# A linear-attention and MLP kernel on one core: exponentials and logarithms by halves of the heads, and another order of the whole program

## The chip, the core and the metric

The kernel runs on one core of one Trainium2 chip. The core has a matrix engine (PE, whose weight loads the profile lists apart as PEld), a vector engine (DVE), an activation engine (ACT), a general engine (POOL) and a sequencer that issues transfers (SP). They run side by side and wait for each other through semaphores. The metric is the time of one execution on the device in microseconds (us), as the median of several runs.

## The reference

Two stages follow each other. The first is a gated linear attention over 4 batches, 8 heads, 768 steps and 48 channels a head; the second is an MLP with SiLU over the 3072 tokens that the first gives, with 384 columns and 2048 hidden units.

```python
f = 1.0 / (1.0 + np.exp(-f_logit))
for t in range(S):
    state = f[:, :, t, :, None] * state + np.einsum('bhd,bhe->bhde', k[:, :, t], v[:, :, t])
    y[:, :, t] = np.einsum('bhd,bhde->bhe', q[:, :, t], state)
# y as x: (tokens, H*D)
h = x @ w_in
g = h * (1.0 / (1.0 + np.exp(-h)))
return g @ w_out
```

## The kernel before

**Tiling.** The 768 steps are cut into 6 chunks of 128, so that there are 24 units (a chunk of a batch, all 8 heads), and two units make a pair. Pairs 0 to 2 are "blocks": their two units are two neighbouring chunks of one batch, and their f, k and q are loaded with two neighbouring steps in one row of 96 numbers. Pairs from 3 on are two batches of the same chunk, loaded in rows of 48.

**A unit's work.** The logits are loaded (`f`), put through exp (`E`) and ln (`L`), so that `lf` holds log(1+exp(-logit)). A matmul with a triangle of ones sums them along the steps (`csh` for a block, `cs` for a unit). From the sums ACT makes `ia` and `a` (exponentials of both signs) and `al` (the decay over the whole chunk). Products with them give scaled keys and queries (`ki`, `qg`), in `qk`. These are turned: in the early units on PE (`tq`, with copies `qc`, `kc` or `qkc`), later by a transposing DMA (`qkD`). `sc2` makes the scores of a pair, `at` masks them on DVE, `vb` casts the values, and `y` is the output: masked scores times values plus queries times the state of the chunk before. `d`, `sd` and `su` carry the state on (for blocks `dT` and `kn` turn the keys back first). `yc` copies y out, `yT` and `xc` (or the transposing DMA `yD`) turn it for the MLP.

**The MLP.** For the first units (`mi1`, `si1`) a matmul group makes 4 tiles of 128 hidden units for one unit, later (`mi`, `si`) 2 tiles for a pair; SiLU runs on ACT. `mo` is a quarter of the second matmul, `oc` copies the output and `so` stores it; the last pair is done by halves of the columns (`moh`, `och`, `soh`). The weights come in pieces: `wi_0` and `wi_1` are 256 columns of w_in each (384 KB), `wi_2` to `wi_4` 512 columns (768 KB), `wo_0` to `wo_3` a quarter of w_out each (768 KB). Every piece is cast to bf16 by three casts (`wic`, `woc`), two for the small ones. `mi1_u_0` needs `wi_0` and `wi_1`, `mi1_u_1` needs `wi_2`, `mi1_u_2` and `mi1_u_3` need `wi_3` and `wi_4`.

**Order.** Nothing is scheduled at build time. A table `PLAN` of some 890 words says, for all engines together, in what order the instructions are issued; a word is the task with its numbers, the engine, and the buffers that it takes (`mi1_0_1/PE/6`: first matmul of unit 0, hidden tiles 4 to 7, on PE, into bank 6 of the eight PSUM banks). Each engine works through its own words in that order and stands still at a word whose inputs or buffers aren't free. `idle_...` words are matmuls of zeros that only keep PE running before there is work. ACT loads another table of functions wherever the plan goes from exponentials to SiLU or back, which it does 17 times in both versions. Line 257 issues f, k, q and v on SP, line 295 w_in and line 299 w_out; line 264 is `E`, lines 266 and 268 `L`; lines 335 to 339 `csh`; line 313 `mi1`, line 323 `mi`, line 351 `mo`, line 357 `moh`; line 280 the scores; line 407 `qkD`, line 442 `yD`; lines 235, 237 and 239 are copies and casts on ACT, DVE and POOL, line 242 the products.

Of the kernel before, what the change touches and what calls it, by code (L numbers as in the profile page):

```python
# [36 lines left out]
kn_0/ACT/0 d_0/PE/2 wi_1/SP/0 wi_0/SP/1 at_0_1/DVE/0 at_0_0/DVE sd_0/DVE/0 at_1_0/DVE/1 su_0/POOL/0 idle_4_2_256/PE/1 y_0/PE/3 tq_3/PE/1,5
idle_5_2_256/PE/2 tq_2/PE/2,0 wo_0/SP/1 a_4/ACT/1 ia_5/ACT/1 al_4/ACT/2 kc_3/ACT/1 at_1_1/DVE qc_3/DVE vb_1/ACT/1 a_5/ACT/2 yc_0/ACT/0 ia_4/ACT/2
kc_2/DVE qc_2/DVE y_1/PE/7 dT_2/PE/5 yT_0/PE/1 sc2_1/PE/6,0,3,2 wo_1/SP/2 wic_2_2/POOL wic_2_0/POOL yc_1/DVE/1 wic_2_1/ACT vb_2/ACT/2 xc_0/DVE/0
at_2_0/DVE/2 at_2_1/DVE dT_1/PE/4 yT_1/PE/7 dT_3/PE/1 mi1_0_1/PE/6 wi_4/SP/3 y_2/PE/0 xc_1/ACT wic_1_0/ACT wic_0_0/ACT kn_1/DVE/1 kn_2/DVE/0  # L40
yc_2/DVE/2 at_3_0/DVE/3 wic_1_1/POOL wic_0_1/POOL mi1_1_1/PE/7 d_2/PE/4 yT_2/PE/5 mi1_0_0/PE/0 mi1_1_0/PE/3 wi_3/SP/4 si1_0_1/ACT/0 si1_1_0/ACT
si1_0_0/ACT sd_2/DVE/1 xc_2/DVE/1 woc_0_2/DVE woc_0_1/DVE woc_0_0/DVE v_3/SP woc_1_2/DVE mi1_2_1/PE/4 mi1_2_0/PE/5 mo_1_0/PE/6 mo_0_0/PE/3 d_1/PE/0
si1_2_1/ACT/1 si1_2_0/ACT kn_3/ACT/0 woc_1_0/POOL si1_1_1/ACT wic_4_0/POOL wic_4_1/POOL wic_4_2/ACT at_3_1/DVE woc_1_1/DVE su_2/DVE/0 wic_3_1/DVE
sd_1/DVE/0 wic_3_2/POOL mo_2_0/PE/4 q_4_5/SP/2 k_4_5/SP/2 mo_1_1/PE mo_0_1/PE mo_2_1/PE mi1_0_3/PE/5 mi1_2_3/PE/1 mi1_1_3/PE/2 wo_2/SP/0 wic_3_0/ACT
vb_3/POOL/3 mi1_1_2/PE/7 y_3/PE/0 si1_0_3/ACT si1_2_3/ACT si1_1_2/ACT yc_3/DVE/0 qg_4/POOL/4 wo_3/SP/1 mi1_2_2/PE/5 d_3/PE/1 ki_4/POOL sd_3/DVE/1
yT_3/PE/7 mi1_0_2/PE/0 si1_2_2/ACT si1_0_2/ACT xc_3/DVE tq_4/PE/5,1 mi1_3_3/PE/7 mi1_3_2/PE/0 kc_4/ACT/2 si1_1_3/ACT qc_4/DVE si1_3_3/ACT si1_3_2/ACT
qg_5/DVE/0 ki_5/POOL tq_5/PE/5,1 mi1_3_0/PE/2 mi1_3_1/PE/7 f_6/SP/3 v_4/SP/2 f_8_9/SP/0 v_5/SP f_7/SP qc_5/ACT si1_3_0/ACT si1_3_1/ACT woc_2_2/POOL
woc_2_0/DVE woc_2_1/DVE kc_5/DVE mo_2_2/PE sc2_2/PE/0,5,2,1 dT_4/PE/7 mo_0_2/PE at_5_1/DVE/0 su_3/DVE/0 su_1/DVE/0 kn_4/DVE/1 at_5_0/DVE at_4_0/DVE/1
# [482 lines left out]
```

## Time and profile before

| what | before |
|---|---|
| median of 3 runs | 177.57 us (177.55 to 178.02) |
| the profiled execution's own time | 177.89 us |
| its span in the trace | 176.1 us |
| PE busy | 169.5 us, 96% of the span |
| ACT busy | 133.3 us, 76% |
| DVE busy | 97.7 us, 55% |
| POOL busy | 59.1 us, 34% |
| table loads on ACT | 17 of 1.28 us |
| moved by DMA | 35.17 MB, of 115541 packets |

The span lies inside the profiled execution: 1.8 us of its time are around it. Busy time counts instructions that were under way, so that a PE that is busy 96% need not run at its peak; where PE waits is read from the starts of its instructions, and what ended a wait from the profile's releasers.

### The profile page before, as it was taken

How to read it: one execution, taken by the hardware profiler on the slowest of the kernel's cores; microseconds unless marked ns; L12 is line 12 of the kernel's file. 1: busy time of each engine (PE TensorE's matmuls, PEld its weight loads, DVE VectorE, ACT ScalarE, POOL GpSimd, SP SyncE). 2: the span in 40 equal slices, each digit the busy share in tenths (PEclk: the TensorE clock that was granted, in tenths of full speed). 3: DMA queues.
4: the chain of work that ended last, by engine and by line, in shares of the span. 5: the costliest groups of instructions: out<-in, count | busy, mean ns of one | idle time of the engine just before them, and what ended most of it. 6: DMA issues, size and time to landing. Idle time of an engine off the chain costs nothing.

```text
span 176.1 us, 4798 instructions
## 1 busy us (share of the span) xinstructions
PE 169.5 (96%) x1952; PEld 133.6 (76%) x1952; DVE 97.7 (55%) x201; ACT 133.3 (76%) x249; POOL 59.1 (34%) x91
## 2 busy tenths in 40 slices
...
DMA  5999998998999999999899994999675975950222
GB/s 147 325 286 259 397 387 220 397 207 169 217 199 241 182 238 221 159 233 232 152 197 165 251 227 89 273 176 210 137 153 99 206 162 138 217 147 0 92 90 89
DMA packets 115541, 35.17 MB, mean 200 GB/s; under 512 B 110752, under 2 KB 113056, under 8 KB 115520
## 3 DMA queue, kind: packets, MB, share of 16 engines
...
## 4 chain that ended last, share of the span: by engine, by line
PE 73%; SPq 8%; DMA 8%; DVE 5%; issue 2%; POOL 2%; ACT 0%; POOLq 0%; DVEq 0%
PE ps L351 27%; PE ps L323 22%; PE ps L313 8%; SPq L257 6%; DMA wh<-in_moe_w_in_dram 5%; PE ps L280 3%; PE ps L357 3%; DMA qkT<-qk 3%; PE ps L426 2%; SPq L442 2%; DVE st L242 2%; PE ps L422 2%; PE ps L372 1%; DVE at L416 1%; PE ps L448 1%
## 5 line engine op out<-in xcount | busy, mean ns | idle before, releaser
L351 PE MATMUL ps<-w_out,hT 128*128 128x384 bf16 x352 | 66.4, 326 | 0.0
L323 PE MATMUL ps<-xT,w_in 128*128 128x256 bf16 x432 | 52.4, 273 | 0.0
L323 PEld LDWEIGHTS <-w_in 128*128 128x128 bf16 x432 | 45.3, 110 | 3.9 <-DMA xT<-yb 0.3
L320 ACT ACTIVATE hT<-ps 128x512 bf16<-128x512 f32 x72 | 39.0, 603 | 10.3 <-PE ps L323 9.6
L351 PEld LDWEIGHTS <-hT 128*128 128x128 bf16 x352 | 31.7, 97 | 16.6 <-ACT hT L310 0.3
L416 DVE TENSOR_TENSOR at<-ps,triu 128x512 bf16<-128x512 f32 x36 | 22.5, 683 | 19.8 <-PE ps L280 18.8
L242 POOL TENSOR_TENSOR qk<-q,av 128x384 bf16<-128x384 f32 x15 | 15.4, 1033 | 42.2 <-DMA q<-in_q_dram 25.0
L499 ACT ACT_TABLE_LOAD x17 | 21.8, 1283 | 0.3
L313 PE MATMUL ps<-xT,w_in 128*128 128x128 bf16 x288 | 17.9, 219 | 0.9 <-POOL w_in L239 0.6
L313 PEld LDWEIGHTS <-w_in 128*128 128x128 bf16 x288 | 16.6, 110 | 1.3 <-POOL w_in L239 0.8
L242 POOL TENSOR_TENSOR qk<-k,ia 128x384 bf16<-128x384 f32 x12 | 12.7, 1066 | 13.4 <-DMA k<-in_k_dram 8.7
L381 ACT ACTIVATE av<-ps 128x384 f32<-128x384 f32 x24 | 11.9, 504 | 3.5 <-PE ps L376 1.8
L237 DVE CAST yb<-ps 128x384 bf16<-128x384 f32 x16 | 8.8, 555 | 10.2 <-PE ps L426 9.0
L264 ACT ACTIVATE f<-f 128x768 f32<-128x768 f32 (+1 forms) x13 | 10.3, 796 | 5.4 <-DMA f<-in_f_logit_dram 5.3
L310 ACT ACTIVATE hT<-ps 128x512 bf16<-128x512 f32 x24 | 13.2, 607 | 1.6 <-PE ps L313 1.5
L453 DVE TENSOR_TENSOR sd<-ps,st 128x384 f32<-128x384 f32 x16 | 8.8, 553 | 9.5 <-ACT hT L320 4.7
L369 POOL DMA_DIRECT2D out_dram<-ob x14 | 8.0, 573 | 17.9 <-DVE ob L237 14.3
L242 POOL TENSOR_TENSOR st<-sd,al 48x192 bf16<-48x192 f32 x18 | 9.8, 543 | 8.7 <-PE ps L422 5.1
L379 ACT ACTIVATE ia<-ps 128x384 f32<-128x384 f32 x24 | 11.8, 505 | 0.0
L237 DVE COPY ob<-ps 128x384 f32<-128x384 f32 x14 | 7.7, 553 | 7.4 <-PE ps L351 3.6
L239 POOL CAST vb<-v 128x384 bf16<-128x384 f32 x11 | 5.6, 507 | 14.6 <-DMA v<-in_v_dram 13.2
L242 DVE TENSOR_TENSOR qk<-k,ia 128x384 bf16<-128x384 f32 x12 | 7.1, 605 | 5.1 <-ACT ia L379 4.2
...
## 6 DMA issues: line engine op xcount, KB each, us to landing
...
```

What stands on the lines that cost most here:

```text
L237: nc.vector.tensor_copy(o, i)
L242: (nc.vector if eng == "DVE" else nc.gpsimd).tensor_mul(*a)
L257: nc.sync.dma_start(out=dst, in_=src)
L310: return nc.scalar.activation(at("hT", u // 2)[:, 4 * m:4 * m + 4, i * C:(i + 1) * C], h, AF.Silu)
L313: nc.tensor.matmul(h[:, n, :], w_in_tile(4 * m + n, kk), at("xT", u // 2)[:, kk, i * C:(i + 1) * C], start=(kk == 0), stop=(kk == KT - 1))
L320: return nc.scalar.activation(at("hT", P)[:, 2 * j:2 * j + 2, :], h, AF.Silu)
L323: nc.tensor.matmul(h[:, i, :], w_in_tile(2 * j + i, kk), at("xT", P)[:, kk, :], start=(kk == 0), stop=(kk == KT - 1))
L351: nc.tensor.matmul(o, at("hT", P)[:, n, i * C:(i + 1) * C], w_out_sb[n // 4][:, n % 4, :], start=(n == 0), stop=(n == NT - 1))
L379: nc.scalar.activation(at("ia", u).rearrange("p h d -> p (h d)"), at("cs", u)[:, 0:HD], AF.Exp)
L381: nc.scalar.activation(at("av", u).rearrange("p h d -> p (h d)"), at("cs", u)[:, 0:HD], AF.Exp, scale=-1.0)
L416: nc.vector.tensor_mul(at("at", u)[:, r], at(f"s{r}", u).rearrange("p (n c) -> p n c", c=C), (triup if two else triu)[:, None, :].to_broad ...
L499: nc.scalar.preload_act_table_set(turn[n])
```

## The change

Three things change in the code. First, the constant `HALF = 3` (the first three pairs are blocks) becomes a set `BLOCKS = {0, 1, 2}` with the same meaning. Second, two new kinds of task, `Eh` and `Lh`, do the exp and the ln of a block for four of the eight heads at a time; all three blocks use them, where one instruction did all heads before. Third, the plan is another one from its first word to its last. Code for transfers of half a block, for weights cast by a DMA of POOL and for the scores of a single unit (`sc`) comes in as well, but no word of the new plan uses it: each block of f is still one transfer. The buffers (`SLOTS`) are the same. The new plan has 10 `E` and 10 `L` of the old form and 6 `Eh` and 6 `Lh`.

```diff
-HALF = 3
+BLOCKS = {0, 1, 2}
...
-f_0_1/SP/0 f_2_3/SP/1 k_0_1/SP/0 q_0_1/SP/0 E_0_1/ACT L_0_1/ACT/0 E_2_3/ACT idle_0_11_512/PE/0 csh_0/PE/0,1 f_4_5/SP/2 q_2_3/SP/1 v_0/SP/0 k_2_3/SP/1
...
+wi_1/SP/1 dT_0/PE/5 kn_0/DVE/0 al_2/ACT/1 dT_2/PE/7 at_0_1/DVE vb_2/ACT/2 d_0/PE/1 Eh_4_1/ACT sd_0/DVE/0 idle_5_2_256/PE/2 y_0/PE/2 qc_3/ACT
...
-        "L": lambda: [(("lf", P), "lf")],
+        "L": lambda: [(("lf", P), "lf")], "Lh": lambda: [(("lf", P), "lf")],
...
-        if u // 2 < HALF and n == 2:
-            dst = at(x, u // 2).rearrange("p a h d -> p (a h d)").rearrange("p (h w) -> p h w", h=H)
-            src = SRC[x][b, :, c * C:(c + 2) * C, :].rearrange("h (p s) d -> p h (s d)", s=2)
+        if u // 2 in BLOCKS and n >= 2:
+            hs = slice(0, H) if n == 2 else slice(4 * us[2], 4 * us[2] + 4)
+            dst = at(x, u // 2).rearrange("p a h d -> p (a h d)").rearrange("p (h w) -> p h w", h=H)[:, hs]
+            src = SRC[x][b, hs, c * C:(c + 2) * C, :].rearrange("h (p s) d -> p h (s d)", s=2)
...
+    def half_logs(kind, u, hf):
+        P, hs = u // 2, slice(4 * hf, 4 * hf + 4)
+        if kind == "Eh":
+            e = at("f", P).rearrange("p a h d -> p (a h d)").rearrange("p (h w) -> p h w", h=H)[:, hs]
+            nc.scalar.activation(e, e, AF.Exp, scale=-1.0)
+        else:
+            nc.scalar.activation(at("lf", P)[:, :, hs, 0:D], pairs("f", P)[:, :, hs], AF.Ln, bias=1.0)
...
+        if kind in ("Eh", "Lh"):
+            return half_logs(kind, *a)
```

**SP, the opening.** The names are buffers: `f0` to `f2`, `k0`, `q0` and so on hold the blocks, `v0` and `v1` single units of v, `wh` the small pieces of w_in, `ws` the large ones. Before, the transfers start so:

```order
L257 DMA f0_69<-in_f_logit_dram 128x8x96
L257 DMA f1_70<-in_f_logit_dram 128x8x96
L257 DMA k0_73<-in_k_dram 128x8x96
L257 DMA q0_77<-in_q_dram 128x8x96
L257 DMA f2_71<-in_f_logit_dram 128x8x96
L257 DMA q1_78<-in_q_dram 128x8x96
L257 DMA v0_81<-in_v_dram 128x8x48
L257 DMA k1_74<-in_k_dram 128x8x96
L257 DMA v1_82<-in_v_dram 128x8x48
L257 DMA v0_81<-in_v_dram 128x8x48
L295 DMA ws0_85<-in_moe_w_in_dram 128x3x512
L295 DMA wh0_90<-in_moe_w_in_dram 128x3x256
```

The next row is `wh1`, which holds `wi_0`; then w_out begins. And now:

```order
L313 DMA wh0_90<-in_moe_w_in_dram 128x3x256
L259 DMA f0_69<-in_f_logit_dram 128x8x96
L259 DMA f1_70<-in_f_logit_dram 128x8x96
L259 DMA k0_73<-in_k_dram 128x8x96
L259 DMA q0_77<-in_q_dram 128x8x96
L259 DMA k1_74<-in_k_dram 128x8x96
L259 DMA q1_78<-in_q_dram 128x8x96
L259 DMA f2_71<-in_f_logit_dram 128x8x96
L259 DMA v0_81<-in_v_dram 128x8x48 x2
L259 DMA v1_82<-in_v_dram 128x8x48
L313 DMA ws0_85<-in_moe_w_in_dram 128x3x512
L313 DMA wh1_91<-in_moe_w_in_dram 128x3x256
```

The small piece `wi_0` has moved from behind the blocks to the front of everything; `wi_1` (now `wh1`) still follows `wi_2`. Behind it now come `wi_3`, `wi_4`, `wo_0`, `wo_1`, where `wo_0`, `wo_1`, `wi_4`, `wi_3` came before.

**POOL, the casts of the first weights** (between the first products and the casts of w_out). Before:

```order
L242 TENSOR_TENSOR st00_146<-sd0_122,al1_125 48x4x48 x2
L239 CAST w_in2_160<-ws0_85 128x512 x2
L239 CAST w_in1_159<-wh0_90 128x384
L239 CAST w_in0_158<-wh1_91 128x384
L239 CAST w_out1_164<-ws2_87 128x512
```

and now:

```order
L243 TENSOR_TENSOR st00_146<-sd0_122,al0_124 48x4x48 x2
L240 CAST w_in2_160<-ws0_85 128x512
L240 CAST w_in1_159<-wh1_91 128x384 x2
L243 TENSOR_TENSOR st10_147<-sd1_123,al1_125 48x4x48 x2
L240 CAST w_in3_161<-ws1_86 128x512
```

Of each small piece ACT made one half and POOL the other; now both halves of `wi_1` are cast on POOL, one behind the other, and both halves of `wi_0` on DVE, earlier.

**DVE, the stretch around pair 2** (masked scores `at`, states `sd` and `st`, where a `st` row x2 is `su`). Before:

```order
L416 TENSOR_TENSOR at0_115<-ps1_62,triup_157 128x512
L242 TENSOR_TENSOR st10_147<-sd1_123,al0_124 48x4x48 x2
L242 TENSOR_TENSOR st00_146<-sd0_122,al1_125 48x4x48 x2
L237 COPY kn1_133<-ps7_68 128x512
L416 TENSOR_TENSOR at0_115<-ps2_63,triup_157 128x512
L416 TENSOR_TENSOR at1_116<-ps0_61,triup_157 128x512
L416 TENSOR_TENSOR at1_116<-ps5_66,triup_157 128x512
L237 CAST vb5_111<-v2_83 128x384
L237 COPY ob0_134<-ps3_64 128x384
L455 COPY sd1_123<-ps2_63 128x384
L242 TENSOR_TENSOR st20_148<-sd1_123,al2_126 48x4x48 x2
```

and now:

```order
L436 TENSOR_TENSOR at0_115<-ps6_67,triup_157 128x512
L436 TENSOR_TENSOR at0_115<-ps2_63,triup_157 128x512
L436 TENSOR_TENSOR at1_116<-ps4_65,triup_157 128x512
L436 TENSOR_TENSOR at1_116<-ps0_61,triup_157 128x512
L238 COPY kn1_133<-ps6_67 128x512
L475 COPY sd1_123<-ps4_65 128x384
L238 COPY ob0_134<-ps1_62 128x384
L238 CAST yb2_121<-ps0_61 128x384
```

The four products of `at` now follow each other, and the three updates `su` of this stretch are on POOL.

On PE, before the first group that needs `wi_0` and `wi_1` (`mi1_0_0`), the old plan has `mi1_0_1 y_2 mi1_1_1 d_2 yT_2`, the new one `d_1 y_1 d_2 mi1_0_1 y_2 yT_1`: `mi1_1_1` and `yT_2` now come after `mi1_0_0`, `d_1` before it.

More of the change, by code (lines that the diff above doesn't have):

```diff
@@ L37 @@
[L37 to L48, printed above, removed]
@@ new lines @@
+qg_0/DVE/0 a_1/ACT/1 ki_1/DVE/1 ia_0/ACT/1 v_1/SP/0 ia_2/ACT/2 qg_1/DVE a_3/ACT/2 ki_2/DVE/2 idle_2_4_512/PE/4 tq_1/PE/4,5 a_2/ACT/0 v_0/SP ki_0/DVE
+kc_1/ACT/0 qc_1/DVE idle_3_4_256/PE/1 tq_0/PE/6,7 qg_2/DVE al_0/ACT/0 v_2/SP/1 kc_0/ACT qc_0/DVE qg_3/POOL/3 idle_4_2_256/PE/0 tq_2/PE/1,4 ia_3/ACT/0
+wi_2/SP/0 sc2_0/PE/5,0,6,7 qc_2/ACT/1 ki_3/DVE kc_2/ACT vb_1/POOL/0 at_0_0/DVE/0 tq_3/PE/3,1 Eh_4_0/ACT dT_1/PE/4 at_1_1/DVE/1 kc_3/ACT vb_0/POOL/1
+wi_1/SP/1 dT_0/PE/5 kn_0/DVE/0 al_2/ACT/1 dT_2/PE/7 at_0_1/DVE vb_2/ACT/2 d_0/PE/1 Eh_4_1/ACT sd_0/DVE/0 idle_5_2_256/PE/2 y_0/PE/2 qc_3/ACT
```

146 lines of the change are left out of this document (82 added, 64 removed).

## The prediction

> **What bounds the kernel now.** I read the page first, then the busy time by stages, then the chain of waits.
>
> ```profile
> span 176.1 us, 4798 instructions
> PE 169.5 (96%) x1952; PEld 133.6 (76%) x1952; DVE 97.7 (55%) x201; ACT 133.3 (76%) x249; POOL 59.1 (34%) x91
> DMA  5999998998999999999899994999675975950222
> ```
>
> PE is the one engine near its span; ACT has 43 us free. The DMA engines are nearly full until some 115 us. The busy time by stages (span, then PE, PEld, DVE, ACT, POOL, clock, DMA share, GB/s) splits this:
>
> ```profile
> 0.00:21.30 21.30, 18.22 (x211) 11.31 (x211) 14.77 (x45) 15.94 (x32) 9.05 (x21) 1.00 0.99 278
> 21.30:40.00 18.70, 18.53 (x266) 15.51 (x267) 11.34 (x25) 14.94 (x26) 8.95 (x13) 1.00 0.99 305
> 40.00:119.00 79.00, 78.77 (x918) 63.23 (x918) 50.20 (x97) 68.53 (x130) 32.24 (x46) 1.00 1.05 202
> 119.00:173.00 54.00, 53.98 (x561) 43.51 (x561) 21.38 (x37) 33.59 (x62) 8.89 (x12) 1.00 0.61 135
> 173.00:176.20 3.20, 0.00 (x0) 0.00 (x0) 0.00 (x0) 0.32 (x1) 0.00 (x0) 0.97 0.29 92
> ```
>
> From 21.3 to 173.0 us PE is busy in 151.3 of 151.7 us at full clock. Before that it is busy too, but partly with matmuls of zeros. So the end is: the moment at which PE has MLP work for good, plus the work then left, plus late starts in between, plus 3.2 us of last copy and store. The chain of waits says what sets that moment (start, duration):
>
> ```profile
> 12.18 0.50 SPq L295
> 12.72 8.02 DMA wh<-in_moe_w_in_dram
> 20.77 0.52 ACT w_in L235
> 21.34 2.85 PE ps L313 x48
> ...
> 173.02 0.32 ACT ob L235
> ```
>
> It is the landing of the last small piece of w_in (12.72 + 8.02 = 20.74), its cast, and the first group that needs it, at 21.34.
>
> **The change part by part.** *The opening.* `wi_0` (384 KB) is now ahead of the first logits. What it costs there is seen by bounds. The timeline of the opening before:
>
> ```profile
> 4.21 0.84 ACT L264 ACTIVATE f<-f 128x768 f32<-128x768 f32 x1 [2.19 <-DMA f<-in_f_logit_dram]
> 5.08 0.84 ACT L266 ACTIVATE lf<-f 128x768 bf16<-128x768 f32 x1
> 7.44 0.85 ACT L379 ACTIVATE ia<-ps 128x384 f32<-128x384 f32 x2
> 8.18 0.49 ACT L381 ACTIVATE av<-ps 128x384 f32<-128x384 f32 x1
> 19.67 0.51 ACT L235 CAST w_in<-wh 128x384 bf16<-128x384 f32 x1 [0.51 <-DMA wh<-in_moe_w_in_dram]
> 19.70 0.51 POOL L239 CAST w_in<-wh 128x384 bf16<-128x384 f32 x1 [0.79 <-DMA wh<-in_moe_w_in_dram]
> 20.80 0.51 POOL L239 CAST w_in<-wh 128x384 bf16<-128x384 f32 x1 [0.60 <-DMA wh<-in_moe_w_in_dram]
> ```
>
> The two small pieces landed 1.10 us apart (19.67 and 20.77, each ending a wait of ACT). At the other end SP needs 0.50 us to issue one (12.18). DMA was full in this stage, so I take 1.10: the first logits come at 5.3 instead of 4.2, and everything of the attention's opening slides by about as much.
>
> *Halves.* A block's logits are still one transfer, so no half starts earlier. What halving saves is the wait of `L` for its `E`: whole, the pair runs from 4.21 to 5.92, 1.71 us. Instructions of 384 columns start 0.37 us apart (7.44, two of them, then 8.18) and last 0.49; four halves take 3 x 0.37 + 0.49 = 1.60. That is 0.11 gained a block, against the 1.10 lost. The Trainium skill, "ScalarE: Activation LUTs" (What ACT_TABLE_LOAD costs), speaks against halves: 186 ns a piece plus 0.833 ns an element, with 93 ns of overlap back to back. By it, an estimate, four halves would take 1.75 us and lose 0.04; the rows with 0.37 say otherwise, and the sum would be worse by 0.15 us if the page held.
>
> *When the MLP starts.* `wi_1` now takes the place of the last small piece: the same bytes stand ahead of it (blocks, single v, `wi_0`, `wi_2`) as stood ahead of `wi_0`, so it lands at 20.77; counted from its own landing before, 19.67 + 1.10 gives 20.77 too. Its two casts are both on POOL, 2 x 0.51, to 21.79, and with the 0.06 between cast and matmul (21.28 to 21.34) `mi1_0_0` starts at 21.85: **0.51 us later**. The attention doesn't hide or add anything to this: `mi1_0_1` before it waits for DVE's cast of `wi_2`, which stands behind five `at` products, and by the 1.1 us of delay and the rows of DVE below I get 20.5 for its start and 21.6 for the end of `y_2` and `yT_1`, 0.2 before the cast is there. If that estimate were off by more than 0.2 us, the attention would set the start.
>
> *Work left then.* The next rows of the chain give each kind's pace on PE:
>
> ```profile
> 24.19 1.30 PE ps L351 x8
> 28.31 2.68 PE ps L313 x48
> 55.06 0.55 PE ps L280 x16
> 62.57 3.27 PE ps L323 x30
> 69.13 0.17 PE ps L422 x4
> 69.30 0.20 PE ps L426 x8
> 160.17 0.34 PE ps L434 x6
> 169.02 3.97 PE ps L357 x48
> ```
>
> `mo` takes 0.65, `mi1` 0.67 (2.68 / 4), `mi` 0.65, a `sc2` 0.55, `y` 0.37, `yT` 0.17, `moh` 0.33. At 21.34 the old plan has `mi1_1_1` and `yT_2` behind it, the new one still ahead; it has done `d_1` in exchange (0.17 like its four-matmul neighbour L422). So **0.67 us** more is left. The kernel does the same matmuls otherwise.
>
> *The rest of the order.* Left at 21.34: 88 `mo` (57.2), 72 `mi` (47.1), 22 `mi1` (14.7), 16 `moh` (5.3), 10 `sc2` (5.5), 21 `y` (7.5), 13 `yT` (2.2), and states, sums and turned keys at the same paces (9.8, an estimate): 149.3 us, in 151.7. So 2.4 us are late starts, and that is all that any order can win there. One place is seen in DVE's rows, with the transposes on PE that wait behind it:
>
> ```profile
> 32.89 0.91 PE L395 MATMUL ps<-ident,qk 128*128 128x128 bf16 x8
> 38.78 1.50 DVE L242 TENSOR_TENSOR st<-sd,al 48x192 bf16<-48x192 f32 x4
> 40.77 1.89 DVE L416 TENSOR_TENSOR at<-ps,triup 128x512 bf16<-128x512 f32 x3
> 43.88 1.11 DVE L242 TENSOR_TENSOR st<-sd,al 48x192 bf16<-48x192 f32 x2
> ```
>
> Four state updates stand between the `at` products there (1.50 us), and two before the turned y. The new plan puts all of these on POOL, which relieves DVE by 2.6 us; PE was covered by `mo` groups in most of this stretch, so I count no more than 0.5 of it. Elsewhere the plan moves work towards ACT and DVE, away from POOL:
>
> ```profile
> L242 POOL TENSOR_TENSOR qk<-k,ia 128x384 bf16<-128x384 f32 x12 | 12.7, 1066 | 13.4 <-DMA k<-in_k_dram 8.7 <-ACT ia L379 3.2 <-ACT av L381 1.4
> L242 DVE TENSOR_TENSOR qk<-k,ia 128x384 bf16<-128x384 f32 x12 | 7.1, 605 | 5.1 <-ACT ia L379 4.2 <-DMA k<-in_k_dram 0.8
> L235 ACT COPY xT<-ps 128x384 bf16<-128x384 bf16 x4 | 1.9, 503 | 0.9 <-PE ps L434 0.9
> ```
>
> Seven `ki` and five `qg` go from POOL (1.07) to DVE (0.60), six `su` the other way. ACT gets four copies of x, four of the output, five of turned keys and queries, and loses four casts of w_in: a net 3 to 5 us at 0.5 each, in the 10 us that it has free between 40 and 119 us (79.0 - 68.5). The cover is thinner, not gone; where it goes, SiLU is late next and holds a PSUM bank. I can't price this other than by its bounds: 2.4 us won (every late start gone) or 2.4 lost (as many again). I take 0, since both plans keep ACT and PE equally close.
>
> **Sum:** 0.51 + 0.67 - 0.0 = 1.2 us on the span, 176.1 to 177.3; around the span nothing changes. The profiled execution took 177.89, 0.3 above the median 177.57, and I add to the median: **178.8 us**.
>
> **The rivals.**
>
> *Late transposes before the last scores, slower still.* The rows of the DMA that turns queries and keys, of PE behind it, and of SP near the end:
>
> ```profile
> 114.22 4.71 DMA qkT<-qk
> 118.97 0.62 PE ps L280 x16
> 143.22 2.48 SPq L442 DMA_TRANSPOSE xT<-yb  x2
> 147.38 3.07 SPq L407 DMA_TRANSPOSE qkT<-qk  x2
> 154.14 0.62 PE L280 MATMUL ps<-qkT 48*128 48x128 bf16 x16
> ```
>
> SP issues in order, and in both plans the last two `qkD` (L407) stand behind `yD_21` (L442), so behind `y_21`. Between `y_21` and the last scores the old plan has 9 `mo` and 8 `mi` on PE, 11.1 us; the new one has 7 and 5, 7.8 us. The way there is 0.7 (copy of y), 1.24 (issue of `yD_21`), 1.24 to 1.83 (first `qkD`), then 4.71 to landing: 7.9 to 8.5. That is 0.1 to 0.7 more than PE has work for: 178.8 + 0.7 = 179.5. Against it: any lateness of PE ahead of `y_21` moves both. Chance 0.10.
>
> *The first piece is nearly free, no change.* If `wi_0` delays only by its issue, 0.50, `wi_1` lands at 20.17 and `mi1_0_0` starts at 21.25, 0.09 earlier than before; 0.67 - 0.09 = 0.58 is left, and DVE's relieved stretch gives 0.5 of it back: 177.6. For it: 0.7 us of the slide is a guess about transfers that overlap. Against: a DMA share of 0.99. Chance 0.22.
>
> *The late starts go, faster.* The mechanism is the interior order alone: the DVE stretch at 38 to 46 us and the places like 32.89, where a group of eight transposes took 0.91 instead of 0.6. If all 2.4 us come back, 1.2 - 2.4 gives 176.4. It decides from 1.7 us regained on (1.2 + 0.5). For it: no engine but PE is full in any stage. Against: the gaps are spread in tenths over 150 us, and a new order makes its own. Chance 0.22.
>
> **How the numbers follow.** A measurement of this kernel can tell about 0.3%, 0.53 us, from no change. The forecast has 0.46, with its own range 178.1 to 179.4 (0.58 to 1.77 on the median: the first piece for its issue alone, or the whole opening with PE's start moved by 1.10 + 0.67). Slower is it and the late transposes, 0.56; no change 0.22, faster 0.22. For 8 in 10 the range reaches down towards the faster case and up to a forecast with most of the 2.4 lost: 176.7 to 181.0.
>
> **What would show it.** First `E` half at 5.2 to 5.4; the two halves of `wi_1` cast on POOL one behind the other, from 20.8; the first `mi1_0_0` near 21.85; PE's share between that and the last matmul at 99% again; the last scores starting right at a landing of `qkT`. A first MLP group before 21.3, or PE's last matmul less than 151.2 us after `mi1_0_0`, would make the forecast wrong.

## The result, and the profile after

The changed kernel takes **180.72 us** as the median of 4 runs (179.01 to 182.04); the kernel before, measured beside it, 177.71 (177.55 to 178.02). The ratio is 1.0105, with a 95% interval of 1.0057 to 1.0153: slower by about 1%, which is 1.9 us (1.0 to 2.7). The medians, which are of all runs, would give 1.017; the ratio leaves out the run of 182.04 us, which counts as a slow one. Forecast were 178.8 us and a range of 176.7 to 181.0, with slower as the likeliest.

The profiled execution of the changed kernel happens to be its longest, 182.04 us, so that some of its waits may be longer than in the median run; where that matters, a later profile of nearly the same kernel (experiment 3, 180.81 us) stands beside it.

The first lines of the page and the busy time by stages (span, then PE, PEld, DVE, ACT, POOL, clock, DMA share, GB/s), with the first cut at the start of `mi1_0_0` again:

```profile
span 180.2 us, 4832 instructions
PE 171.4 (95%) x1965; PEld 135.2 (75%) x1965; DVE 95.3 (53%) x199; ACT 137.3 (76%) x262; POOL 51.8 (29%) x87
```

```profile
0.00:22.35 22.35, 19.23 (x213) 12.09 (x214) 15.11 (x46) 16.19 (x37) 6.84 (x19) 1.00 0.97 275
22.35:40.00 17.65, 16.12 (x243) 14.02 (x240) 8.11 (x16) 14.16 (x29) 5.02 (x7) 1.00 0.88 287
40.00:119.00 79.00, 78.03 (x928) 61.71 (x926) 49.30 (x94) 68.40 (x132) 27.94 (x43) 1.00 1.05 197
119.00:177.10 58.10, 58.03 (x592) 47.37 (x590) 22.84 (x45) 38.26 (x68) 12.04 (x20) 1.00 0.63 139
177.10:180.20 3.10, 0.00 (x0) 0.00 (x0) 0.00 (x0) 0.29 (x1) 0.00 (x0) 0.88 0.30 96
```

The span is longer by 4.1 us (180.2 - 176.1). The first stage is 1.05 us longer (22.39 instead of 21.34), the tail is as it was. The rest lies between: PE now stands still for 1.5 us before 40 us and for 1.0 us between 40 and 119 us, where before it lost 0.2 and 0.2. The waits of PE from 20 to 178 us name the places (line, what it waited for, us in total, times, longest). Of the kernel before:

```profile
PE ps L313 <- ACT w_in L235: 0.3, 1, 0.3
```

and of the changed kernel:

```profile
PE ps L415 <- DVE qk L243: 1.1, 1, 1.1
PE ps L290 <- ACT ob L236: 0.8, 1, 0.8
PE ps L331 <- ACT xT L236: 0.6, 1, 0.6
PE ps L371 <- ACT hT L328: 0.5, 1, 0.5
PE ps L341 <- ACT av L401: 0.2, 1, 0.2
```

L415 (`tq_4`, at 35.7 us) goes back to `q_4_5`, which landed at 35.0 instead of 31.0. L371 (`mo_2_0`) goes back to the first piece of w_out, which landed at 28.8: ACT casts it ahead of the SiLU whose bank `mo_2_0` takes. In the later profile `q_4_5` lands at 31.9 and that piece at 26.5, and both waits are missing, so they belong to this long execution. L290 is the scores of pair 5, at 77.8 us, and L341 the next `mi` group; these two come back in every profile of this order that leaves the place alone.

The opening shows the first term. Rows of its timeline up to `mi1_0_0`:

```profile
1.19 5.89 PE L303 MATMUL ps<-zero 128*128 128x512 bf16 x17 [1.19 <-DVE zero L497]
...
5.44 0.94 ACT L276 ACTIVATE f<-f 128x384 f32<-128x384 f32 x2 [3.42 <-DMA f<-in_f_logit_dram]
...
7.25 0.32 PE L355 MATMUL ps<-lf,tri 128*128 128x384 bf16 x1 [0.17 <-ACT lf L278]
...
20.15 0.62 ACT L236 CAST w_in<-ws 128x512 bf16<-128x512 f32 x1 [1.28 <-DMA ws<-in_moe_w_in_dram]
20.67 0.58 ACT L236 COPY xT<-ps 128x384 bf16<-128x384 bf16 x1
21.20 0.96 POOL L240 CAST w_in<-wh 128x384 bf16<-128x384 f32 x2 [0.34 <-DMA wh<-in_moe_w_in_dram]
21.31 0.83 PE L331 MATMUL ps<-xT,w_in 128*128 128x128 bf16 x12 [0.55 <-ACT xT L236]
...
22.03 0.36 PE L446 MATMUL ps<-vb,at 128*128 128x48 bf16 x8
22.23 0.33 PE L454 MATMUL ps<-ident,yb 128*128 128x128 bf16 x3
22.39 0.83 PE L331 MATMUL ps<-xT,w_in 128*128 128x128 bf16 x12
```

The logits are there at 5.42 (4.19 before), the first sums `csh_0` start at 7.25 (5.98), and the first group of the MLP, `mi1_0_1`, at 21.31 (18.96). The last small weight piece `wi_1` is cast at 22.16, but PE comes to `mi1_0_0` only behind `mi1_0_1`, `y_2` and `yT_1`, at 22.39. So the cast of `wi_1` doesn't set the start; what `mi1_0_1` waits for does, and in this execution two things come to almost the same moment. One is a weight after all, the large piece `wi_2`, which stands behind all the loads of the opening. It landed at 20.13, and at 17.61 before, where POOL took it up:

```profile
17.74 1.17 POOL L239 CAST w_in<-ws 128x512 bf16<-128x512 f32 x2 [1.98 <-DMA ws<-in_moe_w_in_dram]
```

Now ACT waits 1.28 us for it, and behind its cast stands the copy of x that ends PE's wait of 0.55 (20.67 to 21.25). The other is the attention: DVE casts its part of `wi_2` behind the masked scores and is done at 21.14. In the profiles of experiments 1 and 3 `wi_2` landed at 19.84 and 19.53, and there DVE, behind the masked scores, came last.

### The profile page after: what moved, and what is told of

It is laid out like the page before. It is cut to its first block, busy times and chain, and to the rows that moved or that the text cites. A ratio compares the mean times of both kernels' runs of the same rounds, so it can differ in the third digit from the quotient of the medians.

```text
span 180.2 us, 4832 instructions
## 1 busy us (share of the span) xinstructions
PE 171.4 (95%) x1965; PEld 135.2 (75%) x1965; DVE 95.3 (53%) x199; ACT 137.3 (76%) x262; POOL 51.8 (29%) x87
## 4 chain that ended last, share of the span: by engine, by line
PE 68%; SPq 14%; DMA 9%; ACT 6%; issue 1%; DVE 0%; DVEq 0%; ACTq 0%
PE ps L371 27%; PE ps L341 23%; SPq L259 11%; DMA q<-in_q_dram 5%; PE ps L331 5%; DMA f<-in_f_logit_dram 4%; PE ps L377 3%; PE ps L290 2%; SPq L313 2%; PE ps L446 2%; PE ps L442 2%; PE ps L468 1%; ACT hT L338 1%; PE ps L392 1%; ACT av L401 1%
## 5 line engine op out<-in xcount | busy, mean ns | idle before, releaser
L371 PE MATMUL ps<-w_out,hT 128*128 128x384 bf16 x352 | 64.9, 326 | 0.5 <-ACT hT L328 0.5
L341 PE MATMUL ps<-xT,w_in 128*128 128x256 bf16 x432 | 52.0, 273 | 0.2 <-ACT av L401 0.2
L338 ACT ACTIVATE hT<-ps 128x512 bf16<-128x512 f32 x72 | 38.4, 608 | 14.1 <-PE ps L341 13.7
L341 PEld LDWEIGHTS <-w_in 128*128 128x128 bf16 x432 | 44.8, 110 | 3.5 <-issue 0.7
L371 PEld LDWEIGHTS <-hT 128*128 128x128 bf16 x352 | 32.4, 98 | 18.3 <-issue 0.6
L436 DVE TENSOR_TENSOR at<-ps,triu 128x512 bf16<-128x512 f32 x36 | 22.7, 682 | 14.3 <-PE ps L290 13.1
L243 POOL TENSOR_TENSOR st<-sd,al 48x192 bf16<-48x192 f32 x30 | 16.8, 559 | 26.1 <-DVE sd L473 21.7
L243 POOL TENSOR_TENSOR qk<-q,av 128x384 bf16<-128x384 f32 x10 | 11.2, 1127 | 22.5 <-DMA q<-in_q_dram 13.9
L238 DVE COPY ob<-ps 128x384 f32<-128x384 f32 (+1 forms) x13 | 6.6, 506 | 20.5 <-PE ps L371 7.3
L238 DVE CAST yb<-ps 128x384 bf16<-128x384 f32 x15 | 8.2, 554 | 10.3 <-PE ps L446 10.2
L328 ACT ACTIVATE hT<-ps 128x512 bf16<-128x512 f32 x24 | 12.7, 610 | 0.3 <-PE ps L331 0.2
L243 DVE TENSOR_TENSOR qk<-k,ia 128x384 bf16<-128x384 f32 x19 | 11.2, 597 | 3.0 <-ACT ia L399 1.5
L243 DVE TENSOR_TENSOR qk<-q,av 128x384 bf16<-128x384 f32 x14 | 8.4, 618 | 7.5 <-DMA q<-in_q_dram 7.4
L303 PE MATMUL ps<-zero 128*128 128x512 bf16 (+1 forms) x39 | 9.7, 392 | 1.2 <-DVE zero L497 1.2
```

Of the source, the lines that this page charges most:

```text
L238: nc.vector.tensor_copy(o, i)
L243: (nc.vector if eng == "DVE" else nc.gpsimd).tensor_mul(*a)
L328: return nc.scalar.activation(at("hT", u // 2)[:, 4 * m:4 * m + 4, i * C:(i + 1) * C], h, AF.Silu)
L338: return nc.scalar.activation(at("hT", P)[:, 2 * j:2 * j + 2, :], h, AF.Silu)
L341: nc.tensor.matmul(h[:, i, :], w_in_tile(2 * j + i, kk), at("xT", P)[:, kk, :], start=(kk == 0), stop=(kk == KT - 1))
L371: nc.tensor.matmul(o, at("hT", P)[:, n, i * C:(i + 1) * C], w_out_sb[n // 4][:, n % 4, :], start=(n == 0), stop=(n == NT - 1))
```

## The experiments

**How they are read.** From each profile come two numbers: the start of `mi1_0_0` and the end of the last matmul. The work between them I take as 149.4 us with the old split, 0.1 above the sum in the prediction, and as 150.1 with the new one (0.67 more behind the start). What is left of the difference is **late starts**: before 172.98 - 21.34 - 149.4 = 2.2, after 177.03 - 22.39 - 150.1 = 4.5. They are a remainder: of the 2.2 us before, the rows of the prediction show PE standing still for only 0.4 (18.70 - 18.53, 79.00 - 78.77, 54.00 - 53.98), and the rest lies in the paces. So only their differences count, and start, work left and late starts give the end of the last matmul by definition. Each profile is also one execution: the same opening gave starts of 20.66, 20.84, 21.00 and 21.66 in experiments 6, 8, 9 and 10. All words below are words of the plan; "both mends" means the opening and the interior together. Each ratio is to the kernel before on the same chip, with its 95% interval.

**1. The changed kernel once more.** Nothing is edited.

> The changed kernel once more, unchanged. Its four runs lay between 179.0 and 182.0 us where those of the kernel before lay within 0.5, and its profile is of the longest of them. Theory A (the opening: the weights' piece ahead of the logits and 0.67 us of MLP work left over set the loss, the interior is as good as before): the spread is chance, and an ordinary profile shows the first group that needs the piece wi_1 (mi1_0_0) 0.5 to 1.1 us later than before and no wait of PE over 0.5 us behind it. Theory B (the interior: the new order uses transfers just as they land, so that PE waits for DMA in places where the old order had room): the spread comes back, and PE waits for a landing by 0.5 us or more in at least one place after mi1_0_0, first of all at tq_4, which waits for q of pair 2, and at sc2_5, which waits for the turned keys of pair 5.

It took 181.09 us (178.87 to 182.52, 12 runs) against 177.81, ratio 1.0131 (1.0092 to 1.0170). So the slowdown is real. The spread came back, but the kernel before spread nearly as much on this chip (177.14 to 180.37 in 25 runs), so the spread doesn't tell the theories apart. The profile is again of the longest run (182.52 us). In it the logits land at 5.88, `csh_0` starts at 7.80, `mi1_0_0` at 22.79, and the late starts are 4.6. The delay of the logits isn't a constant: 1.2 us in one profile and 1.7 in the other. As theory B has it, PE waits for over 0.5 us behind `mi1_0_0`, at `sc2_5` (1.1) and at `sc2_4` (0.6); the wait at `tq_4` is gone.

**2. Halves alone.** The kernel before with its own order, every `E` and `L` of a block replaced by two halves:

```diff
-f_0_1/SP/0 f_2_3/SP/1 k_0_1/SP/0 q_0_1/SP/0 E_0_1/ACT L_0_1/ACT/0 E_2_3/ACT
+f_0_1/SP/0 f_2_3/SP/1 k_0_1/SP/0 q_0_1/SP/0 Eh_0_1/ACT Eh_0_0/ACT Lh_0_1/ACT/0 Lh_0_0/ACT Eh_2_1/ACT Eh_2_0/ACT
```

> The order before, with the exponentials and logarithms of the three blocks by halves of the heads in the places where the whole ones stood; nothing else moved. By the rows of before a block gains 0.11 us in the opening, which the wait for the weights at 21.3 us hides: theory A and theory B both expect no change, 177.3 to 177.9 us. If the page's rule of 186 ns a piece held, at most 0.15 us would be lost, which is no change either. Over 178.2 or under 177.0 would say that the halves do something that neither theory knows.

It took 178.12 us, ratio 0.9990 (0.9957 to 1.0023): nothing that can be measured. Its first rows on ACT:

```profile
4.18 0.94 ACT L276 ACTIVATE f<-f 128x384 f32<-128x384 f32 x2 [2.17 <-DMA f<-in_f_logit_dram]
5.03 0.92 ACT L278 ACTIVATE lf<-f 128x384 bf16<-128x384 f32 x2
```

Four halves run from 4.18 to 5.95, 1.77 us, where the whole pair took 1.71. They lose 0.06 a block instead of gaining the 0.11 of the prediction. The rows that the prediction took 0.37 and 0.49 from, 0.86 for two, are of exps that read the sums in `ps`; these read `f`, and two of them need 0.92 to 0.94. By the rule of the Trainium skill, "ScalarE: Activation LUTs" (What ACT_TABLE_LOAD costs), the prediction estimated 1.75 us for the four, and the 1.77 of this run agree with it.

**3. The new order with whole `E` and `L`.**

```diff
-Eh_0_1/ACT Eh_0_0/ACT k_2_3/SP/1 Lh_0_1/ACT/0 Lh_0_0/ACT
+E_0_1/ACT k_2_3/SP/1 L_0_1/ACT/0
```

and likewise for the other two blocks.

> The new order with whole exponentials and logarithms of the blocks in the places of the last half; nothing else moved. By the rows of before the opening loses 0.11 us a block, of which the first two lie on the way to the first sums. The logits land at 5.4 to 5.9 and the fillers hold PE until 7.2: 0 to 0.3 us slower than the new order. By the run with the halves in the old order (0.999 of before, interval 0.996 to 1.002) no difference that can be measured.

It took 180.96 us (180.76 to 182.29), ratio 1.0177 (1.0145 to 1.0210), and its interval overlaps with that of experiment 1. Neither direction shows a gain or a loss by halves; the loss is in the order. This profile is the 180.81 us one spoken of above: `csh_0` 7.42, `mi1_0_0` 22.89, last matmul 175.76, late starts 175.76 - 22.89 - 150.1 = 2.8.

**4. The piece of weights alone.** The kernel before with its own order, `wi_0` moved to the front:

```diff
+wi_0/SP/1 f_0_1/SP/0 f_2_3/SP/1 k_0_1/SP/0 q_0_1/SP/0
...
-wi_0/SP/1
```

> The order before with the piece wi_0 moved to the front of SP's queue; nothing else. Theory A: the logits land 1.1 us later, wi_1 is now the last small piece and lands where wi_0 did, at 20.7; the attention's slide is partly covered by the 1.2 us that the first MLP group waited for its weights before. 177.6 to 178.6 us. Theory B: the opening is covered wholly by the wait for the weights, 177.4 to 177.9 us.

It took 179.38 us (178.44 to 180.01), ratio 1.0069 (1.0034 to 1.0104). Both theories had less, 178.6 at most. So this one move costs 0.7%. Its first row of `E`:

```profile
6.26 0.84 ACT L264 ACTIVATE f<-f 128x768 f32<-128x768 f32 x1 [4.24 <-DMA f<-in_f_logit_dram]
```

and the stages 6 to 12 and 12 to 21 us (last column GB/s):

```profile
6.00:12.00 6.00, 4.00 (x40) 2.20 (x38) 1.97 (x4) 5.68 (x12) 0.00 (x0) 1.00 1.04 275
12.00:21.00 9.00, 7.57 (x125) 5.57 (x122) 8.14 (x16) 6.84 (x16) 5.61 (x8) 1.00 1.00 277
```

The same stages of the kernel before:

```profile
6.00:12.00 6.00, 5.85 (x59) 3.27 (x60) 3.61 (x7) 5.97 (x14) 1.62 (x3) 1.00 1.18 311
12.00:21.00 9.00, 7.74 (x145) 6.42 (x142) 8.05 (x16) 6.65 (x16) 5.55 (x9) 1.00 1.03 308
```

The logits came 2.05 us later than before (6.24 against 4.19). `mi1_0_0` started at 23.83, 2.49 later, but the last matmul ended only 1.68 later (174.66): late starts fell from 2.2 to 1.4. Part of a late opening is given back further on; that everything PE waits for there has more time is the likely reason, but not a shown one. Not only the 384 KB stand ahead: from 6 to 21 us the transfers moved 275 to 277 GB/s instead of 308 to 311. Why the rate is lower isn't shown.

The rows of POOL and of PE say what the late start waited for:

```profile
20.69 1.17 POOL L239 CAST w_in<-ws 128x512 bf16<-128x512 f32 x2 [2.60 <-DMA ws<-in_moe_w_in_dram]
...
21.91 0.86 PE L313 MATMUL ps<-xT,w_in 128*128 128x128 bf16 x12 [1.50 <-POOL w_in L239]
```

It is `wi_2`, which landed at 20.57 instead of 17.61, and not the attention: PE stood 1.50 us ahead of `mi1_0_1` until POOL had cast it. A piece at the front delays the weights that stand last in the queue as well as the logits.

**5. The new order with the piece behind the blocks.**

```diff
-wi_0/SP/0 f_0_1/SP/0 ... wic_0_1/DVE ... wic_0_0/DVE
+f_0_1/SP/0 ... wi_1/SP/1 wi_0/SP/0 ... wic_0_1/DVE wic_0_0/DVE mi1_0_0/PE/5
```

> The new order with the weights' piece wi_0 put back behind wi_1 on SP, and its two casts put on DVE just ahead of the first group that needs them. Theory A: the logits land 1.1 to 1.2 us earlier, at 4.2 us, the first group that needs both small pieces starts 0.3 to 0.8 us earlier, and the time falls by as much. Theory B: the transfers behind the weights land when they did, so the waits of the interior stay where they are in time, and the time falls by less than 0.3 us.

It took 180.98 us, ratio 1.0153 (1.0107 to 1.0198): no better than the changed kernel, though the logits were early again (4.12). Its rows show why:

```profile
1.19 6.28 PE L303 MATMUL ps<-zero 128*128 128x512 bf16 x17 [1.19 <-DVE zero L497]
...
4.98 0.92 ACT L278 ACTIVATE lf<-f 128x384 bf16<-128x384 f32 x2
...
7.31 0.33 PE L355 MATMUL ps<-lf,tri 128*128 128x384 bf16 x1
...
21.73 1.08 DVE L238 CAST w_in<-wh 128x384 bf16<-128x384 f32 x2
22.86 0.84 PE L331 MATMUL ps<-xT,w_in 128*128 128x128 bf16 x12 [0.93 <-DVE w_in L238]
```

`lf` is done at 5.90, but the new order has 17 matmuls of zeros on PE ahead of `csh_0` (the old one 11), which hold it until 7.3. And the casts of `wi_0`, now on DVE behind two updates of states, end at 22.8. This run didn't undo one part, it traded one wait for two; it says nothing on the piece by itself.

**6. The opening mended.** So the fillers and the casts' engines have to go with the piece:

```diff
-wi_0/SP/0 f_0_1/SP/0 ... idle_0_17_512/PE/0 ... wic_0_1/DVE ... wic_0_0/DVE
+f_0_1/SP/0 ... idle_0_11_512/PE/0 ... wi_1/SP/1 wi_0/SP/0 ... wic_0_0/ACT wic_1_1/POOL wic_0_1/POOL
```

> The new order with its opening mended: wi_0 behind wi_1 on SP, 11 instead of 17 matmuls of zeros before the first sums (in the run with the piece put back these 17 kept PE until 7.3 us, though the logarithms were done at 5.9), and the two casts of wi_0 on POOL and ACT instead of DVE. Theory A: mi1_0_0 starts at 21.3 to 21.8 instead of 22.4 to 22.8, and the time falls by 0.8 to 1.4 us. Theory B: the opening is made up for by waits that shorten further on (sc2_5 waits longer), and less than 0.4 us is won.

`csh_0` starts at 6.02, `mi1_0_1` at 19.12, and `mi1_0_0`

```profile
20.66 0.85 PE L331 MATMUL ps<-xT,w_in 128*128 128x128 bf16 x12 [0.19 <-ACT w_in L236]
```

2.2 us earlier than in experiment 3 and 0.7 earlier than before the change. The last matmul, though, ended at 175.16, only 0.6 earlier than in experiment 3: the late starts had risen from 2.8 to 4.4. The time was 180.06 us, ratio 1.0100 (1.0070 to 1.0131). Experiment 3, which ran on the same chip and differs besides only by whole `E` and `L`, has 1.0145 to 1.0210, so that the mended opening shows in the times too; against experiment 1, on another chip, the intervals overlap. Three of the waits:

```profile
PE ps L290 <- DMA qkT<-qk: 0.8, 1, 0.8
PE ps L290 <- ACT ob L236: 0.7, 1, 0.7
...
PE ps L341 <- ACT av L401: 0.2, 1, 0.2
```

The second and third are those of pair 5 again. The first is at the scores of pair 4: PE now comes to them at 68.05, and half of them must wait for the transposed unit 9 until 69.30. With the late opening PE came to them later, at 71.27 and without a wait in the changed kernel's first profile; in that of experiment 1 it waited there for 0.6.

**7. The interior mended.** In the changed kernel's profile ACT and PE show what holds the scores of pair 5:

```profile
76.56 0.84 ACT L266 ACTIVATE f<-f 128x768 f32<-128x768 f32 x1 [2.17 <-DMA f<-in_f_logit_dram]
77.31 0.46 ACT L236 COPY ob<-ps 128x384 f32<-128x384 f32 x1
77.82 0.62 PE L290 MATMUL ps<-qkT 48*128 48x128 bf16 x16 [0.80 <-ACT ob L236]
```

ACT stands 2.17 us at `E_14_15`, for logits of a pair that is needed much later. Behind it is `oc_6`, whose PSUM bank the scores take. (In the profile of experiment 3 it stood 1.88 us, and the scores waited 0.51.) The transposed unit 10 landed only at 77.47 as well, since `qkD_10` stood behind `f_14_15` on SP and its `ki_10` behind `sd_5` on DVE. The edit:

```diff
-qkD_11/SP/2 ... d_5/PE/4 si_3_4/ACT f_14_15/SP/3 mo_7_1/PE sd_5/DVE/1 ... ki_10/DVE ... qkD_10/SP
+vb_8/DVE/0 ki_10/DVE ... qkD_11/SP/2 ... d_5/PE/4 si_3_4/ACT mo_7_1/PE sd_5/DVE/1 ... qkD_10/SP f_14_15/SP/3
...
-E_14_15/ACT y_9/PE/3 oc_4/DVE/3 ... oc_6/ACT/4 ... L_14_15/ACT/1
+y_9/PE/3 oc_4/DVE/3 ... oc_6/ACT/4 ... oc_7/ACT/2 E_14_15/ACT L_14_15/ACT/1
```

> The new order with one place of the interior changed: ki_10 moved ahead of sd_5 on DVE, the logits f_14_15 moved behind the transpose qkD_10 on SP, and E_14_15 and L_14_15 four tasks later on ACT. In all three profiles of the new order PE waits 0.8 to 1.3 us at sc2_5 for the landing of qkD_10 and 0.36 us at mi_4_7 for a_13 behind L_14_15. Theory B (interior): both waits go, 1.0 to 1.6 us less than the new order. Theory A (opening): PE is only late for later work and the waits come back further on, less than 0.4 us won. Theory C (DMA is full in this stage, so that whatever is put first makes the other late): sc2_5's wait goes but cs_14, cs_15 or mi_4_7 wait longer, 0 to 0.6 us won.

By the order of ACT's own words `E_14_15` comes seven tasks later and `L_14_15` five.

Both waits are gone from the profile; the late starts are 2.2 (last matmul 174.68, start 22.34). The time was 180.07 us, ratio 1.0121 (1.0081 to 1.0162). By times alone it can't be told from the changed kernel, and theory B's 1.0 to 1.6 us don't show; what it shows is in the trace. With the late starts as before, what is left of the loss there is the start (+1.00) and the work left (+0.67): the last matmul ends 1.70 us later than before the change.

**8. Both mends.**

> The two changes together: opening mended and the place at sc2_5 changed. Theories A and B together, each for its part: 1.8 to 3.0 us less than the new order, which is within 0.7 us of the kernel before; the 0.67 us of MLP work that is left over at the start stay. If one of the two explains all, this one is as fast as that one alone.

It took 179.83 us, ratio 1.0109 (1.0068 to 1.0150). That is far from the 1.8 to 3.0 us expected, and no faster than either mend alone (1.0100 and 1.0121): in the times the two don't add up. `mi1_0_0` started at 20.84, the last matmul ended at 174.28, late starts 3.3. The wait of pair 4 was the longest one left:

```profile
68.08 0.40 PE L290 MATMUL ps<-qkT 48*128 48x128 bf16 x8
69.43 0.40 PE L290 MATMUL ps<-qkT 48*128 48x128 bf16 x8 [0.95 <-DMA qkT<-qk]
```

So against the kernel before, the last matmul ends 1.3 us later (174.28 - 172.98): -0.50 by the start, +0.67 by the work left, +1.1 by late starts. Two ways to take the wait away follow.

**9. Unit 9 earlier.** On top of both mends:

```diff
-ia_8/ACT/1 mi_3_3/PE/2 ia_10/ACT/0 ki_8/DVE a_10/ACT/1 ... ia_11/ACT/2 ia_9/ACT/1 ... ki_9/DVE
+ia_8/ACT/1 ia_9/ACT/2 mi_3_3/PE/2 ia_10/ACT/0 ki_8/DVE ki_9/DVE/4 a_10/ACT/1 ... ia_11/ACT/1
```

> The version with both mends, and the keys of unit 9 made earlier: ia_9 right behind ia_8 on ACT (it stood behind ia_10, a_10, a_11, al_8 and ia_11), ki_9 right behind ki_8 on DVE. Theory (the time that is lost behind the opening is the late transposing DMA of unit 9, which the scores sc2_4 wait for): ia_9 ends near 61.3 instead of 62.8, qkD_9 is issued right behind qkD_8, near 63.3 instead of 64.2, and lands near 68.5; the wait inside sc2_4 falls from 1.13 us to 0.2, PE's late starts behind mi1_0_0 from 3.4 to 2.4, its last matmul ends near 173.3 and the median falls by 0.9 to 178.9. Rival (the wait is given back by the next late thing, a SiLU's bank or the scores of pair 5): the wait inside sc2_4 goes, the late starts stay at 3.2 to 3.4, and the median stays at 179.8.

The scores of pair 4 run in one piece:

```profile
68.69 0.62 PE L290 MATMUL ps<-qkT 48*128 48x128 bf16 x16
```

and behind `mi1_0_0` two waits are named, of which the second (0.3) was there in experiment 8 too:

```profile
PE ps L341 <- DVE sd L473: 0.4, 1, 0.4
PE ps L341 <- DMA xT<-yb: 0.3, 1, 0.3
```

`qkD_9` was issued at 63.08 and landed at 66.26 instead of 69.38. Late starts fell from 3.3 to 2.7, not to 2.4: `ki_9` took 1.37 us (61.31 to 62.68) while POOL's product ran from 60.92 to 62.26, `sd_7` waited behind it on DVE, and with it the bank that `mi_3_4` takes (0.54). Time 179.57 us, ratio 1.0075 (1.0041 to 1.0110). The theory holds for its place, with about half of the gain given back at `mi_3_4`, 5.5 us earlier.

**10. The scores of pair 4 later.** On top of both mends:

```diff
-mo_6_0/PE/2 si_3_7/ACT sc2_4/PE/5,6,4,0 ... mo_7_2/PE at_9_0/DVE/0 su_3/POOL/0 mo_6_1/PE
+mo_6_0/PE/2 mo_7_2/PE mo_6_1/PE si_3_7/ACT sc2_4/PE/5,6,4,0 ... at_9_0/DVE/0 su_3/POOL/0
```

> The version with both mends, with two groups of mo (mo_7_2 and mo_6_1, 1.31 us of PE) moved from behind the scores sc2_4 to ahead of them; transfers, ACT and DVE as they were. Theory (PE only stood at the wrong place in its order: it has other work, but behind the scores that wait): sc2_4 starts near 69.4, at the landing of qkD_9, and loses nothing; late starts behind mi1_0_0 2.3 us, last matmul near 173.2, median 178.8. Rival (the scores are what the next work waits for, so that 1.31 us later at the scores is 1 us later at the masks, at y_9 and the turned y of the pair): a wait of about 1 us shows up at y_9 or at the first mi of pair 4, and the median stays near 179.8.

Time 179.30 us, ratio 1.0070 (1.0041 to 1.0099). The wait at the scores is gone, and this line has come:

```profile
PE ps L446 <- DVE at L436: 0.4, 1, 0.4
```

It is 0.55 us at `y_9`, and 0.25 more at `y_8` behind it, so 0.8 of the 1.1 came back, where the rival had 1. The median lies midway between the theory's 178.8 and the rival's 179.8. Late starts 2.8.

**11. Everything found, first form.** Experiment 9 with three more moves: `mi1_1_1` ahead of `mi1_0_0` again, so that its 0.67 us lie in PE's wait for `wi_0`; `sd_7` ahead of `ki_9`; `mo_18_3` ahead of `mi_10_7`.

```diff
-mi1_0_1/PE/2 sd_2/DVE/1 ... y_2/PE/1 a_4/ACT/1 su_2/POOL/0 yT_1/PE/0 yc_2/ACT/2 mi1_0_0/PE/5 xc_1/DVE al_4/ACT/2 yT_2/PE/1 mi1_1_1/PE/6
+mi1_0_1/PE/2 yT_1/PE/0 sd_2/DVE/1 xc_1/DVE ... y_2/PE/1 mi1_1_1/PE/0 a_4/ACT/1 su_2/POOL/0 yc_2/ACT/2 mi1_0_0/PE/5 al_4/ACT/2 yT_2/PE/1
```

In this form two PSUM banks are taken over too early, so that the state of unit 2 and a quarter of unit 1's hidden tiles have other values; the amount of work is that of the others.

> The version with both mends and the earlier keys of unit 9, with three more changes of place, each aimed at one lost stretch of that version. First, mi1_1_1 ahead of mi1_0_0 again, as the old order had it, with yT_1, yc_1 and xc_1 earlier for it (PE waits 0.67 us there for wi_0, so that mi1_0_0 then starts 0.3 later with 0.67 less left behind it: 0.35 won). Second, sd_7 ahead of ki_9 on DVE (mi_3_4 waited 0.54 for its bank). Third, mo_18_3 ahead of mi_10_7 on PE (0.45 of waiting for the turned y of unit 21). Theory (the whole difference between the two orders is the start of the MLP, the 0.67 us left behind it, and waits of this kind at a few places): mi1_0_0 near 21.3, late starts behind it 1.8, last matmul near 172.5, and a median 1.3 us below that version's 179.57, so 178.2, and a ratio to the kernel before of 0.998 to 1.002. Rival (the new order holds a loss that these terms do not show, for instance slower transfers): the terms change as said, but the ratio stays at 1.005 to 1.0075.

Time 178.32 us against 178.35 before, ratio 1.0013 (0.9982 to 1.0044). In its profile `mi1_1_1` starts only at 22.01, because `sd_2`, `yT_1` and `xc_1` wait for each other, and the last matmul ends at 174.54, not at 172.5; that profile, at 179.53 us, is the longest of its runs.

**12. Everything found, second form.** `sd_2` stands ahead of `yT_1`, the banks are exchanged so that none is taken early, and `mi1_0_3` stands ahead of `mo_2_0`:

```diff
-mi1_0_1/PE/2 yT_1/PE/0 sd_2/DVE/1 xc_1/DVE
+mi1_0_1/PE/2 sd_2/DVE/1 yT_1/PE/0 xc_1/DVE
...
-mo_2_0/PE/5 si1_1_2/ACT mo_1_0/PE/3 ... mi1_0_3/PE/4
+mi1_0_3/PE/5 si1_1_2/ACT mo_2_0/PE/4 mo_1_0/PE/3
```

> The version before it showed two of its changes of place spoiled: yT_1 stood ahead of sd_2, so that sd_2, yT_1, xc_1 and mi1_1_1 waited for each other, and mi1_1_1 started at 22.0 instead of 20.7. Here sd_2 stands ahead of yT_1, the banks of mi1_1_1 and of what follows are exchanged, and mi1_0_3 stands ahead of mo_2_0, which waited 0.3 to 0.4 us for the first piece of w_out. Theory (start of the MLP, work left behind it and waits at a few places are the whole difference): mi1_1_1 near 20.7, mi1_0_0 near 21.4, late starts behind it 1.5 to 2.0 us, last matmul 172.3 to 172.9, median 177.5 to 178.2, ratio to the kernel before 0.996 to 1.001. Rival (the new order holds a loss that these terms do not show): the terms come out as said, but the ratio is 1.003 or more.

Time 178.43 us (178.05 to 179.79) against 178.11, ratio 1.0032 (1.0007 to 1.0057). The row of `mi1_1_1` and `mi1_0_0` on PE:

```profile
21.01 1.50 PE L331 MATMUL ps<-xT,w_in 128*128 128x128 bf16 x24 [0.48 <-DVE xT L238]
```

and the stages from 40 us to the last matmul:

```profile
40.00:119.00 79.00, 79.00 (x948) 63.33 (x946) 51.76 (x96) 68.38 (x133) 28.70 (x43) 1.00 1.04 200
119.00:173.20 54.20, 54.17 (x541) 43.87 (x538) 19.41 (x38) 35.39 (x63) 10.61 (x18) 1.00 0.61 138
```

`mi1_0_0` starts at 21.68, 0.3 later than hoped; the last matmul ends at 173.18, late starts are 173.18 - 21.68 - 149.4 = 2.1. In both stages PE is busy in all but 0.03 us. Against the kernel before the two terms are +0.34 and -0.14, +0.20 together, and the ratio says +0.6 us (0.1 to 1.0). By the ratio this is on the rival's side, just; but start and late starts came out 0.3 and 0.1 us worse than the theory had them, and with these 0.4 us (0.2%) its upper end of 1.001 becomes 1.003. The move of `mi1_1_1` won nothing by itself: against experiment 9 `mi1_0_0` starts 0.68 later (21.68 instead of 21.00), with 0.67 less left behind it. The last matmul ends 0.65 earlier because of the late starts, which went from 2.7 to 2.1. Of some 2.3 us (ratio 1.0131) all but 0.6 (ratio 1.0032) is undone by all the moves together, and these two intervals don't overlap. How much each move has of it the times don't tell, and a rest of a few tenths that the terms don't hold is neither shown nor excluded. No version was measurably faster than the kernel before.

## Why the prediction was right, and which terms were wrong

The three terms, in us against the kernel before, by the end of the last matmul in each profile:

| | forecast | changed kernel | with whole `E`, `L` | both mends | all moves |
|---|---|---|---|---|---|
| start of `mi1_0_0` | +0.51 | +1.05 | +1.55 | -0.50 | +0.34 |
| work left behind it | +0.67 | +0.67 | +0.67 | +0.67 | 0 |
| late starts | 0 | +2.3 | +0.6 | +1.1 | -0.1 |
| sum | +1.2 | +4.0 | +2.8 | +1.3 | +0.2 |
| the profiled execution (177.89 before) | | 182.04 | 180.81 | 179.26 | 178.16 |

The column of the changed kernel is of its longest run; by the ratio the kernel lost 1.9 us, not 4.0.

**Direction and size.** The direction is right: the start moved later, though by another path than the forecast's, and 0.67 us more was left behind it. The size was too small: 1.9 us were lost by the ratio and 2.3 in experiment 1, where 1.2 were forecast. The median came out 1.9 us above the forecast and 0.3 below the end of the range; that of experiment 1, 181.09, lies just above it. Two of the three terms were too small. That the range held is in part luck, since its upper end was set for an interior that loses most of 2.4 us, which the prediction couldn't price.

**The opening: mis-sized.** The 1.10 us for the piece ahead of the logits, taken from the gap between two landings, was 1.2 in the first profile, 1.7 in that of experiment 1, 1.3 in experiment 3, 1.6 in experiment 7 and 2.05 in experiment 4. The upper bound of that step, 1.10, wasn't one: the piece's own bytes at the stage's rate (384 KB, 393 thousand bytes, at 275 to 308 GB/s) take 1.3 to 1.4 us.

**What sets the start: the step that failed.** The prediction let the cast of `wi_1` decide (21.85) and estimated the attention's chain to end 0.2 us ahead of it, with the warning that beyond 0.2 us the attention would set the start. It came later: `mi1_0_1`, put at 20.5, started at 21.3 to 21.6 in the three profiles. The cast of `wi_1` ended at 22.16, and PE came to `mi1_0_0` at 22.39 in the changed kernel and at 22.8 to 22.9 in experiments 1 and 3. The prediction had `mi1_0_1` wait for DVE behind the masked scores, which is what ended the wait in experiments 1 and 3. It didn't price the landing of `wi_2`, which slid from 17.61 to between 18.46 and 20.13 in four profiles of this order of transfers, and which in the first profile is level with DVE. From `csh_0` to `mi1_0_1` the new order needs 13.1 us where nothing is late (experiment 6) and 13.4 to 14.2 where the piece is ahead, so the start moves by more than the logits do; and the 17 matmuls of zeros hold PE until 7.1 to 8.0 in these profiles.

**Work left, 0.67: in the plan, not tested by itself.** That `mi1_1_1` stands behind `mi1_0_0` is in the plan's words, and the price is the pace of `mi1` in the profile. The balance can't test it, since the late starts are its remainder, and taking it away in experiment 12 won nothing, because the start moved by as much. In the prediction's sum of the work left, 21 `y` at 0.37 are 7.8 us and not 7.5, so that the 2.4 us of late starts, which bound its interior, would be 2.1.

**Halves: wrong sign, no weight.** -0.11 a block was +0.06, and nothing in the time.

**The interior, taken as 0: wrong.** It was 0.6 us worse in the profile of experiment 3 and 2.3 in that of the longest run; the bound of that step was 2.4. In the profiles of experiments 1, 3, 5 and 6, which leave it alone, the scores of pair 5 and the group behind lost 1.0 to 1.6 us, a stall of ACT and SP in their own order. The cover on ACT that the prediction weighed (79.0 - 68.5) says nothing on that: ACT was idle while it stood there. The relief of DVE between 38 and 46 us, "no more than 0.5", can't be seen beside it.

**The rivals.** *Late transposes before the last scores* named the right kind of wait at the wrong pair: in the first profile `sc2_11` started at 156.21, 0.7 behind its landing, while pairs 4 and 5 lost. *The first piece nearly free* falls with experiment 4, which pays 0.7% for it alone. *The late starts go* fell too: in the new order they came below those of before only with all the moves of experiment 12, by 0.1.

**Signs named ahead.** The first `E` half at 5.2 to 5.4 was at 5.44 and 5.90; the two casts on POOL from 20.8 began at 21.20 and 20.93; `mi1_0_0`, named near 21.85, started at 22.39 and 22.79; the last scores didn't start at a landing. PE at 99% after the start was, in the first profile, 91% up to 40 us and 99% from there on.
